# Row maxima of q transposed by TensorE instead of a DMA, and the first gating product read from SBUF, in a new order of the whole program

## The chip, the cores and the metric

The kernel runs on one core of a Trainium2 chip. The metric is the device time of one execution in microseconds (us), lower is better. Three executions of the kernel before took 317.10, 327.22 and 329.62 us (median 327.22). A profiled execution took 319.29 us, and its span, from the first to the last instruction, is 317.5 us. All durations below are from that profiled execution.

The engines are named as the profile names them: PE is TensorE (PEld its weight load), DVE is VectorE, ACT is ScalarE, POOL is GpSimd, SP is the engine that here only issues DMAs. Each engine executes its own instructions in the order in which they were written and waits, by semaphores, for what the others have to give it first.

## The reference

Two stages: a linear attention with exponential features, and a gated long convolution. Shapes: 8 batches, 8 heads, 576 rows, head width 64; the second stage has 576 rows by 512 channels.

```python
def phi(x):                       # q and k, w_phi is 64 x 128
    proj = x @ w_phi
    proj = proj - max(abs(proj), axis=-1)
    return concat([exp(proj), exp(-proj)])
kv  = phi(k).T @ v;   z = sum(phi(k))
x   = (phi(q) @ kv) / (phi(q) @ z + 1e-6)      # heads side by side: 576 x 512

x1, x2, x3 = split(x @ w_proj)                 # 512 -> 3 x 512
X2  = rfft(x2);  H = rfft(filter)
y   = x1 * irfft(X2 * H) * x3
out = y @ w_out
```

The first step of this change is in `phi(q)`: the maximum of each row has to be subtracted, and on the path of the transposed projection this is done by a matmul whose moving operand holds the maxima transposed. The second is in `X2 * H`, a complex product, of which the real and the imaginary part are each a sum of two products.

## The kernel before, in words

The program is one long list of words, `PLAN` (line 24), run through by `run` (line 967). A word such as `Pq,2,1@4` calls the method `Pq` with batch 2 and index 1 and gives it PSUM bank 4. The list was made by a planner and is the order of the work: each engine gets its instructions in the order of the words, so one word that waits holds everything that stands behind it on its engine. Loads from memory are issued by POOL (`load`, `loadh`, `w_load`), transposes by DMA and stores by SP, so these two queues follow the list as well. DMAs that are in flight at the same time share the 16 DMA engines.

For each of 8 batches the words are, in order of dependence:

- `load` brings q, k and v as bf16; `trh` (line 547) transposes a half of q or k by a DMA of SP. Batch 0 is transposed by PE (`T`, line 562, and `Te`).
- `Pk`, `Qn` and the short `Pkt`, `Qnt` project k and q by rows into PSUM; `maxk`, `maxq`, `maxkt`, `maxqt` reduce them to maxima of absolute values on DVE (line 654). `ex,k` are the exponentials of k on ACT, `em` the exponentials of the maxima of k, which `vs` on POOL multiplies into v; `KV` sums the products with v over the rows.
- The maxima of q take another way. `mhi` (line 674) rounds them to bf16 on ACT, `mlo` (line 677) makes the rest that bf16 lost, on POOL or DVE, both into the tile `mh`; `trm` (line 682) transposes `mh` to `mT` by a DMA of SP. `Pq` and `Pqt` (lines 609 and 624) project q with the features on the partitions and add, by matmuls with the constant `sel`, the negative maxima from `mT` to the same PSUM sums. `ex,q` and `exqt` are the exponentials of that.
- `NE`, `NEt` form numerator and denominator, `rc`, `xn`, `rct`, `xnt` divide on DVE, `trx` and `trxt` transpose the result by DMAs of SP.
- `fold` and `foldt` form even and odd parts for the transform; `X1`, `X2`, `X3` (with `X1t`, `X3t`) are the three projections, `X1e`, `X2e`, `X1te` copy them out of PSUM on ACT or DVE, and `tm`, `tmt` multiply x3 into x1.
- `F` (line 817) is the forward transform of x2, into two banks for index 0 and 1 and one bank for index 4. Two readers take the two banks: `Fe` (line 820) copies them as bf16 to the tile `C`, on ACT or DVE, and `m1` (line 823), always on DVE, multiplies them by the filter's `A` into `Y`. `m2` multiplies the other part of `C` by `B`, `m3` adds or subtracts the two; both are on POOL or DVE.
- `I` is the inverse transform; `Ie`, `Ip`, `Im` combine its halves, `ym` multiplies by x1 and x3, `O` (with `Oa`, `Ob`) is the last projection, `Oe` copies it out and `st` stores it, by two DMAs of SP.

The words of several batches are interleaved. Ahead of the first batch's second stage stand also the filter's transform (`filt_load`, `filt_fold`, `H`, `H_ev`) and the tables of sines (`gen_...`). The helper `port` (line 271) makes a POOL instruction wait for the last DVE instruction ahead of it that was handed to the helper; these are DVE instructions that work from SBUF to SBUF:

```python
        if eng == "DVE":
            self.hold = last or first
        elif eng == "POOL" and self.hold is not None:
            self.tc.add_manual_dep(
```

The functions that the change touches, and their caller:

Of the kernel before, what the change touches and what calls it, by code (L numbers as in the profile page):

```python
# [8 lines left out]
FP32 = mybir.dt.float32  # L9
# [3 lines left out]
ALU = mybir.AluOpType  # L13
# [23 lines left out]
Pq,0,0@0 ex,q,m,0,0@0 Qn,1,1@6 ex,q,p,0,0@0 Pq,0,1@2 ex,q,p,0,1@2 ex,q,m,0,1@2 gen_fwd trh,k,1,1
Pq,0,3@0 gen_fwd5 load,k,2 trh,k,2,1 trh,k,2,0 maxq,1,1@6 NE,0,0@4 ex,q,p,0,3@0 rc,0,0@4 xn,0,0@4
Pkt,1@6 maxkt,1@6 trx,0,0 load,v,1 ex,q,m,0,3@0 NE,0,1@2 rc,0,1@2 xn,0,1@2 trx,0,1 vs,POOL,p,0,1
vs,POOL,m,0,1 KV,0,1@4 KVe,DVE,0,1@4 exkt,m,1@6 exkt,p,1@6 em,m,1,0 Qn,1,0@0 maxq,1,0@0 Pq,0,2@2  # L40
ex,q,m,0,2@2 NE,0,3@4 ex,q,p,0,2@2 rc,0,3@4 xn,0,3@4 Pk,1,2@6 Qnt,1@0 em,p,1,0 w_load,proj,0
maxqt,1@0 mhi,1 filt_fold,POOL,0 Pqt,0@4 exqt,p,0@4 maxk,1,2@6 Pk,1,3@2 trx,0,3 filt_fold,POOL,2
load,q,2 NE,0,2@0 rc,0,2@0 xn,0,2@0 exqt,m,0@4 NEt,0@4 filt_fold,POOL,1 maxk,1,3@2 vs,POOL,m,1,0
H,1@0 ex,k,m,1,2@6 ex,k,p,1,2@6 mlo,POOL,1 trm,1 rct,0@4 xnt,0,0@4 em,m,1,1 xnt,0,1@4 H_ev,DVE,3@0
vs,POOL,p,1,0 gen_inv ex,k,m,1,3@2 H,0@6 H_ev,ACT,1@0 H_ev,DVE,0@6 ex,k,p,1,3@2 KV,1,0@4
KVe,DVE,1,0@4 trx,0,2 fold,POOL,0,1 H_fix H_ev,DVE,2@6 trxt,0 load,q,3 trh,q,2,0 Pq,1,0@0
ex,q,p,1,0@0 ex,q,m,1,0@0 Pq,1,1@2 ex,q,m,1,1@2 ex,q,p,1,1@2 w_load,proj,2 Pk,2,0@4 maxk,2,0@4
foldt,DVE,0,0 H,4@0 H_ev,DVE,4@0 ex,k,m,2,0@4 NE,1,0@6 rc,1,0@6 xn,1,0@6 X1,0,1@1 X1e,DVE,0,1@1
em,p,1,1 X1,0,0@2 X2,0,3@3 ex,k,p,2,0@4 Pk,2,1@6 ex,k,p,2,1@6 Qn,2,1@0 ex,k,m,2,1@6 foldt,POOL,0,1
late X2e,DVE,0,3@3 maxq,2,1@0 X2,0,4@4 X2e,DVE,0,4@4 X2,0,2@3 X2e,ACT,0,2@3 maxk,2,1@6 fold,POOL,0,0  # L50
X2,0,0@5 X2e,ACT,0,5@4 vs,POOL,p,1,1 X2,0,1@0 X1e,ACT,0,0@2 X2e,ACT,0,1@0 X2e,DVE,0,0@5 Qn,2,0@6
maxq,2,0@6 Pqt,1@2 exqt,p,1@2 exqt,m,1@2 trh,q,2,1 Qnt,2@4 maxqt,2@4 F,0,0@0 trh,q,3,0 Fe,ACT,0,0@0
load,k,3 Pkt,2@6 maxkt,2@6 F,0,1@2 X1,0,2@4 exkt,m,2@6 X1e,ACT,0,2@4 exkt,p,2@6 m1,0,0@0 Pq,1,3@0
ex,q,m,1,3@0 NE,1,1@4 Fe,DVE,0,1@2 ex,q,p,1,3@0 vs,POOL,m,1,1 KV,1,1@6 KVe,ACT,1,1@6 m1,0,1@2
em,p,2,0 Qn,2,2@2 rc,1,1@4 xn,1,1@4 maxq,2,2@2 trx,1,0 Pk,2,2@0 ex,k,p,2,2@0 Pq,1,2@4 trh,q,3,1
load,v,2 Qn,2,3@6 maxq,2,3@6 ex,q,m,1,2@4 mhi,2 m2,POOL,0,1 m2,POOL,0,0 X3,0,0@2 tm,0,0@2 X1t,0@3
X1te,ACT,0@3 maxk,2,2@0 F,0,4@6 m1,0,4@6 Pk,2,3@2 maxk,2,3@2 m3,POOL,0,0 ex,q,p,1,2@4 ex,k,m,2,2@0
X1,0,3@7 X1e,ACT,0,3@7 mlo,POOL,2 X3t,0@4 tmt,0@4 X3,0,3@6 tm,0,3@6 NE,1,2@0 rc,1,2@0 m3,POOL,0,1
I,0,0,0@7 vs,POOL,p,2,0 em,m,2,0 vs,POOL,m,2,0 em,p,2,1 vs,POOL,p,2,1 trm,2 ex,k,p,2,3@2 xn,1,2@0
trx,1,1 ex,k,m,2,3@2 NE,1,3@4 rc,1,3@4 trh,k,3,0 xn,1,3@4 X3,0,2@6 Qn,3,3@0 maxq,3,3@0 Ie,0,0@7  # L60
Pq,2,1@2 ex,q,m,2,1@2 ex,q,p,2,1@2 Qnt,3@4 maxqt,3@4 X3,0,1@7 em,m,2,1 Qn,3,0@0 maxq,3,0@0 Pq,2,0@4
ex,q,m,2,0@4 ex,q,p,2,0@4 NEt,1@2 trx,1,2 KV,2,0@0 KVe,ACT,2,0@0 rct,1@2 xnt,1,0@2 xnt,1,1@2 trx,1,3
tm,0,1@7 I,0,0,1@2 Ip,0,0@2 Im,0,0@2 I,0,1,0@3 Ie,0,1@3 tm,0,2@6 Pq,2,2@4 ex,q,p,2,2@4 NE,2,0@0
rc,2,0@0 ex,q,m,2,2@4 xn,2,0@0 vs,POOL,m,2,1 KV,2,1@2 KVe,ACT,2,1@2 trh,k,3,1 fold,DVE,1,1 Pq,2,3@6
ex,q,p,2,3@6 Qn,3,2@0 maxq,3,2@0 trxt,1 ex,q,m,2,3@6 trx,2,0 load,q,4 NE,2,1@4 rc,2,1@4 xn,2,1@4
trx,2,1 X2,1,2@2 X2e,ACT,1,2@2 w_load,out load,k,4 X2,1,3@3 X2e,DVE,1,3@3 I,0,2,0@0 Ie,0,2@0
fold,POOL,1,0 Qn,3,1@6 ym,POOL,0,0 maxq,3,1@6 Pk,3,0@4 ex,k,m,3,0@4 I,0,1,1@1 Ip,0,1@1 Im,0,1@1
X2,1,1@3 X2e,ACT,1,1@3 I,0,3,0@0 I,0,2,1@2 Im,0,2@2 NE,2,3@6 ex,k,p,3,0@4 Ie,0,3@0 X2,1,0@3
X2e,ACT,1,0@3 rc,2,3@6 foldt,POOL,1,0 xn,2,3@6 foldt,POOL,1,1 X2,1,4@1 X2e,ACT,1,4@1 X2e,ACT,1,5@1
Ip,0,2@2 mhi,3 Pqt,2@6 exqt,p,2@6 maxk,3,0@4 I,0,3,1@0 exqt,m,2@6 load,v,3 NE,2,2@2 X1,1,1@1  # L70
ym,POOL,0,1 Ip,0,3@0 Im,0,3@0 ym,POOL,0,2 mlo,DVE,3 F,1,0@4 rc,2,2@2 xn,2,2@2 F,1,4@0 m1,1,4@0
X1e,ACT,1,1@1 Fe,ACT,1,0@4 Pk,3,1@2 ex,k,p,3,1@2 ex,k,m,3,1@2 m1,1,0@4 load,k,5 F,1,1@6 m1,1,1@6
# [111 lines left out]
class Kernel:  # L184
# [824 lines left out]
```

## Time and profile before

| what | before |
|---|---|
| median of three executions | 327.22 us |
| profiled execution, its span | 319.29 us, 317.5 us |
| mean granted clock of PE | 0.946 of full speed |
| busy PE, DVE, ACT, POOL | 278.7, 250.6, 230.3, 220.3 us |
| DMA, mean over the span | 131 GB/s |
| SP's queue: transposes of x, k, q, maxima, rest of x | 32, 14, 14, 8, 8 |
| first matmul of `X2` (line 801) | 62.35 us after the span's start |
| last store issued | 313.27 us |

How to read it. A matmul's end is modelled, and matmuls overlap, so a busy PE can still have small gaps: what a row of matmuls costs is read from the starts. A group's line gives, after the bar, the busy us, the mean ns of one instruction, the idle time of the engine just before them and what ended it. The waits of an engine do no harm where that engine is not what the others wait for.

### The profile page before, as it was taken

To read this page: it belongs to the slowest core of one execution; us is meant where nothing else is said; L and a number is where in the kernel's file an instruction comes from. 1 tells how busy PE (TensorE), PEld (TensorE's weight loads), DVE (VectorE), ACT (ScalarE), POOL (GpSimd) and SP (SyncE) were. 2 spreads that over 40 slices of the span, in tenths; PEclk is the share of its full clock that TensorE was granted. 3 is DMA by queue.
4 is the path that set the end of the run, shared out by engine and by line. 5 is a ranking of instruction groups with operands and counts; after the bars stand their busy time and mean duration, and the time that the engine had idled before them with its cause. 6 is when DMAs were issued, how large, how long until landed. Compare 5 with 4: busy or idle time off the path is not lost.

```text
span 317.5 us, 9411 instructions
## 1 busy us (share of the span) xinstructions
PE 278.7 (88%) x3901; PEld 161.0 (51%) x3901; DVE 250.6 (79%) x415; ACT 230.3 (73%) x363; POOL 220.3 (69%) x171
## 2 busy tenths in 40 slices
PE   0553478899999999999799999999999999999991
PEld 0433365546675546466365555664565554654440
DVE  6994559999987988888679898987898866786750
ACT  5794378989888888885778957798768877635542
POOL 8697914799987786698589868956788566813230
PEclk9955559999999999999999999999999999999997
DMA  6999994899699996999969949565339310360346
GB/s 122 243 214 184 225 216 77 125 163 162 123 150 183 177 141 105 195 76 139 212 134 152 167 67 204 102 115 136 82 46 133 82 35 24 69 119 2 77 95 159
DMA packets 78666, 41.50 MB, mean 131 GB/s; under 512 B 58976, under 2 KB 73440, under 8 KB 78624
## 3 DMA queue, kind: packets, MB, share of 16 engines
q1 hardware_dynamic: 63808, 24.66, 45.3%
q0 software_dynamic: 14816, 16.25, 34.0%
q8 instruction: 30, 0.49, 0.7%
q14 instruction: 12, 0.10, 0.1%
HBM read 33.75 MB, written 9.44 MB: 136 GB/s over the span
## 4 chain that ended last, share of the span: by engine, by line
PE 64%; DMA 12%; DVE 11%; POOL 3%; SPq 3%; issue 3%; ACT 2%; POOLq 0%; DVEq 0%; ACTq 0%
PE ps L844 15%; DMA kT<-kn 9%; PE ps L895 8%; PE ps L801 7%; PE ps L936 7%; PE ps L458 5%; PE ps L709 4%; PE ps L730 4%; DVE mq L654 3%; DMA mT<-mh 2%; PE ps L851 2%; PE ps L587 2%; PE ps L621 2%; PE ps L442 1%; PE ps L615 1%
## 5 line engine op out<-in xcount | busy, mean ns | idle before, releaser
L844 PE MATMUL ps<-xT,wproj 128*128 128x512 bf16 x256 | 64.1, 379 | 0.2 <-DVE mq L654 0.2
L913 POOL TENSOR_TENSOR yT<-cv,x1s 128x576 bf16<-128x576 f32 x27 | 34.3, 1277 | 31.5 <-DVE cv L903 14.5
L654 DVE TENSOR_REDUCE mq<-ps 128x8 f32<-128x1024 f32 (+1 forms) x40 | 43.8, 1110 | 7.8 <-PE ps L594 6.8
L654 DVE TENSOR_REDUCE mk<-ps 128x8 f32<-128x1024 f32 (+1 forms) x40 | 44.2, 1112 | 3.7 <-PE ps L587 1.4
L694 POOL TENSOR_TENSOR vp<-vn,vp 128x1152 bf16<-128x1152 bf16 x16 | 34.4, 2150 | 9.2 <-ACT vp L688 7.1
L638 ACT ACTIVATE Ekm<-ps 128x1024 bf16<-128x1024 f32 x32 | 32.6, 1027 | 9.5 <-PE ps L587 5.8
L694 POOL TENSOR_TENSOR vm<-vn,vm 128x1152 bf16<-128x1152 bf16 x16 | 34.4, 2148 | 7.2 <-ACT vm L688 7.2
L638 ACT ACTIVATE Eqm<-ps 128x1024 bf16<-128x1024 f32 x32 | 32.7, 1025 | 5.1 <-PE ps L621 3.1
L936 PE MATMUL ps<-wout,yT 128*128 128x512 bf16 x144 | 36.2, 379 | 0.1
L832 POOL TENSOR_TENSOR t<-C,B 128x1024 bf16<-128x1024 bf16 x13 | 27.5, 2118 | 12.5 <-ACT C L714 9.5
L895 PE MATMUL ps<-inv,Y 128*128 128x288 bf16 (+1 forms) x192 | 36.0, 289 | 0.0
L638 ACT ACTIVATE Ekp<-ps 128x1024 bf16<-128x1024 f32 x32 | 32.9, 1028 | 3.7 <-DVE mk L654 2.2
L638 ACT ACTIVATE Eqp<-ps 128x1024 bf16<-128x1024 f32 x32 | 32.7, 1025 | 3.6 <-PE ps L621 2.9
L844 PEld LDWEIGHTS <-wproj 128*128 128x128 bf16 x256 | 23.1, 97 | 23.1 <-issue 0.2
L801 PE MATMUL ps<-wproj,eo 128*128 128x512 bf16 x128 | 31.1, 379 | 1.2 <-DVE KVs L716 1.2
L903 DVE TENSOR_TENSOR cv<-es,ps 128x288 f32<-128x288 f32 x64 | 26.5, 448 | 6.5 <-PE ps L895 5.2
L837 POOL TENSOR_TENSOR Y<-Y,t 128x1024 bf16<-128x1024 bf16 x14 | 29.6, 2124 | 2.3 <-DVE Y L827 1.1
L827 DVE TENSOR_TENSOR Y<-ps,A 128x1024 bf16<-128x1024 f32 (+1 forms) x24 | 24.7, 1041 | 4.6 <-PE ps L458 2.1
L881 DVE TENSOR_TENSOR x1s<-ps,x1s 128x512 bf16<-128x512 f32 x32 | 21.7, 686 | 5.1 <-PE ps L844 4.7
L714 ACT COPY o<-ps 128x512 f32<-128x512 f32 x29 | 17.0, 590 | 12.0 <-PE ps L936 7.7
L714 ACT CAST x1s<-ps 128x512 bf16<-128x512 f32 (+1 forms) x30 | 16.6, 552 | 10.3 <-PE ps L844 8.5
L895 PEld LDWEIGHTS <-Y 128*128 128x128 bf16 (+1 forms) x192 | 14.4, 96 | 18.3 <-issue 9.6
(153 smaller groups left out, 634.6 us busy)
## 6 DMA issues: line engine op xcount, KB each, us to landing
out_dram<-o SPq DMA_DIRECT2D x72, 128.0 KB, 2.4
vn<-in_v_dram POOLq DMA_DIRECT2D x8, 576.0 KB, 9.6
kn<-in_k_dram POOLq DMA_DIRECT2D x7, 576.0 KB, 8.6
qn<-in_q_dram POOLq DMA_DIRECT2D x7, 576.0 KB, 8.6
wproj<-in_moe_w_proj_dram POOLq DMA_DIRECT2D x3, 512.0 KB, 8.9
fl<-in_moe_filter_fft_dram SPq DMA_DIRECT2D x18, 64.0 KB, 5.1
kn<-in_k_dram POOLq DMA_DIRECT2D x2, 288.0 KB, 5.8
qn<-in_q_dram POOLq DMA_DIRECT2D x2, 288.0 KB, 7.9
```

The costliest lines, as they stand in the source:

```text
L638: self.nc.scalar.activation(e, self.db(), AF.Exp, bias=0.0, scale=1.0 if g == "p" else -1.0)
L654: self.nc.vector.tensor_reduce(out=out, in_=src, axis=AX.X, op=ALU.max, apply_absolute_value=True)
L694: self.port(eng, self.elem(eng).tensor_tensor(out=t[:, :, :, 0:64], in0=self.at("vn", b)[:, 2 * X:2 * X + 2], in1=t[:, :, :, 64:65].to_bro ...
L714: self.nc.scalar.copy(dst, src)
L801: self.mm(self.pb(0), eo[:, kt, 128 * c:128 * c + 128], w[:, kt, 512:1024], start=(kt == 0), stop=(kt == 3))
L832: self.port(eng, self.elem(eng).tensor_tensor(out=self.at("t2", b)[:, t, :], in0=self.at("C", b)[:, o, :], in1=self.at("B"), op=ALU.mult))
L837: self.port(eng, self.elem(eng).tensor_tensor(out=Y, in0=Y, in1=self.at("t2", b)[:, i:i + 3:2, :], op=ALU.add if i else ALU.subtract))
L844: self.mm(self.pb(0), w[:, kt, f0 + 128 * m:f0 + 128 * m + 128], x[:, kt, :], start=(kt == 0), stop=(kt == 3))
L895: self.mm(self.pb(0, 0, 288), y, t, start=(k == 0), stop=(k == 2))
L903: self.nc.vector.tensor_tensor(out=self.at("cv", 4 * b + m)[:, :, odd, :], in0=e, in1=o, op=ALU.subtract if odd else ALU.add)
L913: self.port(eng, self.elem(eng).tensor_tensor(out=self.at("yT", b)[:, m, 0:SEQ], in0=self.at("cv", 4 * b + m).rearrange("p j h t -> p (j h ...
L936: self.mm(self.pb(0), y[:, kt, 128 * j:128 * j + 128], w[:, kt, :], start=first and kt == ks[0], stop=last and kt == ks[-1])
```

## The change

Three things change at once.

`trm` is replaced by two words. `Tm` is a transpose by PE: a matmul against the identity, out of `mh` into a PSUM bank, like the words `T` that batch 0 uses for q and k. `Tme` copies the result to `mT`, on DVE for batches 0, 1, 2, 4 and 5 and on ACT for 3, 6 and 7.

`m1` of index 0 and 1 reads the copy in `C` instead of the PSUM banks, so it follows `Fe`, and the banks are free after `Fe`; as it has no operand in PSUM any more it may also be on POOL. Of the 16, ten are on DVE and six on POOL. `m1` of index 4 is as before.

The list of words is a new one throughout: 1,451 words instead of 1,443. The engines of many words are others. `Fe` is on ACT 10 times (13 before), `X1e` 19 (25), `X2e` of whole tiles 25 (18); `m2` is on POOL 8 times (13), `m3` 11 (14), `ym` 22 (27), `fold` 10 (8), `mlo` 7 (6). The rings of buffers are as before. Only the start of both lists is shown, up to the first words of batch 0's second stage; the tile of PSUM is called `banks` instead of `ps`.

```diff
 PLAN = """
-w_load,phi zeros w_phi,ACT loadh,k,0,1 gen_rows gen_cols,0 gen_turns,ACT,0 loadh,k,0,0 gen_cols,1
-gen_turns,DVE,1 gen_angles,1 gen_sin,1 gen_angles,0 gen_ident T,k,0,0,0@0 Te,ACT,k,0,0,0@0
...
-filt_load,SP,1 Pk,0,1@6 maxk,0,1@6 Qn,0,1@4 maxq,0,1@4 load,k,1 T,q,0,1,0@0 Te,DVE,q,0,1,0@0
-exkt,m,0@2 Qn,0,0@4 maxq,0,0@4 em,p,0,0 gen_sel T,q,0,1,1@1 Pk,0,3@2 maxk,0,3@2 load,q,1
...
-vs,POOL,m,0,0 KV,0,0@4 gen_five mhi,0 mlo,DVE,0 trm,0 Qn,1,3@0 KVe,DVE,0,0@4 ex,k,m,1,0@6
-ex,k,p,1,0@6 Pk,1,1@2 ex,k,m,1,1@2 ex,k,p,1,1@2 maxq,1,3@0 maxk,1,0@6 maxk,1,1@2 Qn,1,2@4 maxq,1,2@4
-Pq,0,0@0 ex,q,m,0,0@0 Qn,1,1@6 ex,q,p,0,0@0 Pq,0,1@2 ex,q,p,0,1@2 ex,q,m,0,1@2 gen_fwd trh,k,1,1
...
+w_load,phi w_phi,ACT zeros loadh,k,0,0 gen_rows gen_cols,1 gen_turns,DVE,1 gen_angles,1 gen_sin,1
+gen_cols,0 loadh,q,0,0 loadh,q,0,1 loadh,k,0,1 load,v,0 gen_ident T,k,0,0,1@0 filt_load,SP,0
...
+ex,k,p,0,1@0 load,q,1 T,q,0,1,0@6 Te,ACT,q,0,1,0@6 gen_turns,POOL,0 gen_angles,0 Te,DVE,k,0,1,1@5
+maxk,0,0@2 filt_load,SP,1 Pkt,0@4 maxkt,0@4 em,m,0,0 T,q,0,1,1@7 T,q,0,0,1@0 Te,DVE,q,0,0,1@0
+Te,DVE,q,0,1,1@7 Qnt,0@6 em,p,0,0 exkt,p,0@4 trh,q,1,0 exkt,m,0@4 trh,q,1,1 load,k,1 maxqt,0@6
+Qn,0,1@0 maxq,0,1@0 trh,k,1,0 Pk,0,3@2 Pk,0,2@6 ex,k,m,0,2@6 Qn,0,2@4 maxq,0,2@4 ex,k,m,0,3@2
+ex,k,p,0,2@6 gen_pads gen_sin,0 gen_sel gen_selx Qn,0,0@0 maxq,0,0@0 Qn,0,3@4 maxq,0,3@4 mhi,0
+vs,POOL,p,0,0 vs,POOL,m,0,0 maxk,0,3@2 maxk,0,2@6 em,p,0,1 em,m,0,1 mlo,DVE,0 KV,0,0@0 KVe,DVE,0,0@0
+Tm,0@6 ex,k,p,0,3@2 Tme,DVE,0@6 Pq,0,0@6 ex,q,p,0,0@6 ex,q,m,0,0@6 gen_five gen_inv Qn,1,0@0
+maxq,1,0@0 Pq,0,1@4 ex,q,m,0,1@4 ex,q,p,0,1@4 Qn,1,1@2 maxq,1,1@2 Pq,0,2@6 Qnt,1@0 maxqt,1@0
+trh,k,1,1 Qn,1,2@2 maxq,1,2@2 Pqt,0@0 ex,q,p,0,2@6 NE,0,0@4 gen_fwd5 NE,0,1@2 load,q,2 trh,q,2,0
+ex,q,m,0,2@6 exqt,m,0@0 rc,0,0@4 xn,0,0@4 trx,0,0 Pq,0,3@6 trh,q,2,1 Qn,1,3@4 exqt,p,0@0 rc,0,1@2
...
-        self.ps = self.psp.tile([128, 8, 512], FP32, name="ps")
+        self.banks = self.psp.tile([128, 8, 512], FP32, name="banks")
...
-    def trm(self, b):
-        self.nc.sync.dma_start_transpose(
-            out=self.at("mT", b), in_=self.at("mh", b).rearrange("p g h x -> p (g h x)"))
+    def Tm(self, b):
+        self.nc.tensor.transpose(self.turned(1), self.at("mh", b).rearrange("p g h x -> p (g h x)"),
+                                 self.at("ident"))
+
+    def Tme(self, eng, b):
+        self.copy(eng, self.at("mT", b), self.turned(1))
...
-    def m1(self, b, i):
-        t = slice(4, 5) if i == 4 else slice(i, i + 3, 2)
-        p = self.ps[:, self.bank:self.bank + (1 if i == 4 else 2), :]
-        a = {0: slice(0, 2), 1: slice(2, 0, -1), 4: slice(3, 4)}[i]
-        self.nc.vector.tensor_tensor(out=self.at("Y", b)[:, t, :], in0=p, in1=self.at("A")[:, a, :],
-                                     op=ALU.mult)
+    def m1(self, eng, b, i):
+        Y, A = self.at("Y", b), self.at("A")
+        if i == 4:
+            self.nc.vector.tensor_tensor(out=Y[:, 4, :], in0=self.pb(0), in1=A[:, 3, :], op=ALU.mult)
+            return
+        t = slice(i, i + 3, 2)
+        self.port(eng, self.elem(eng).tensor_tensor(
+            out=Y[:, t, :], in0=self.at("C", b)[:, t, :],
+            in1=A[:, slice(2, 0, -1) if i else slice(0, 2), :], op=ALU.mult))
```

Of the rest of the new list, the places that matter below are these. In batches 0 to 2 `Tm` stands right behind `mlo` or one `KV` after it; in the later batches some words of PE lie between them. Behind `Tm` of batch 1 stand `Pk,1,2`, `Qn,2,1` and `H`, behind that of batch 2 `X3`, `X3t` and `Pq`. SP's transposes of q of batch 2 stand ahead of the first `trx` of batch 0. `w_load,proj,1`, the weights of `X2`, is issued behind the loads of q, k and v of batch 2.

## The prediction

> **What bounds the kernel now.** I read the page's busy shares and slices first, then the window table, the chain of waits, and the groups that the change touches.
>
> ```profile
> PE 278.7 (88%) x3901; PEld 161.0 (51%) x3901; DVE 250.6 (79%) x415; ACT 230.3 (73%) x363; POOL 220.3 (69%) x171
> PE   0553478899999999999799999999999999999991
> PEclk9955559999999999999999999999999999999997
> 20.00:50.00 30.00, 16.01 (x321) 12.62 (x320) 17.67 (x26) 17.29 (x23) 19.65 (x15) 0.54 1.22 198
> 60.00:130.00 70.00, 69.44 (x1036) 39.97 (x1037) 62.50 (x100) 60.34 (x96) 59.10 (x42) 1.00 0.98 156
> 150.00:160.00 10.00, 7.68 (x89) 3.78 (x81) 5.49 (x10) 6.69 (x14) 6.17 (x7) 1.00 1.16 218
> 160.00:300.00 140.00, 139.80 (x1866) 78.12 (x1866) 115.27 (x186) 101.00 (x161) 94.96 (x63) 1.00 0.55 96
> ```
>
> A window row gives busy us of TensorE, weight load, VectorE, ScalarE and GpSimd, then granted clock, share of the DMA engines, GB/s. Three stages show. Until about 60 us TensorE is half idle and, from 20 to 50, clocked at 0.54. From 60 to 305 it has no hole but one of 2.3 us at 150:160. The last 12 us are evacuation and stores. To check how full 60 to 305 is I priced TensorE's work from the chain of waits, where four 512-column matmuls in a row take 0.86 us, a KV group 1.16 (72 matmuls in 55.50 to 56.66), an NE group 0.53: about 264 us for the program, 21 of it ahead of the first X2 (62.35 us), 243 behind it. Those 243 took until 311, 249 us. So **only the opening (41 us lost), one hole and the tail can give time**; the middle can only lose.
>
> ```profile
> 31.55 1.19 SPq L683 DMA_TRANSPOSE mT<-mh  x1
> 37.85 0.61 PE L621 MATMUL ps<-mT,sel 64*128 64x128 bf16 x8 [0.46 <-DMA mT<-mh]
>   PE ps L621: 0.7, 2
> DMA to landing us min/median/max: 2.2/3.5/7.2
> L827 DVE TENSOR_TENSOR Y<-ps,A 128x1024 bf16<-128x1024 f32 x16 | 19.3, 1219 | 2.8 <-PE ps L458 2.1 <-ACT C L714 0.6
> L832 DVE TENSOR_TENSOR t<-C,B 128x1024 bf16<-128x1024 bf16 x3 | 2.1, 686 | 0.0
> L837 POOL TENSOR_TENSOR Y<-Y,t 128x1024 bf16<-128x1024 bf16 x14 | 29.6, 2124 | 2.3 <-DVE Y L827 1.1 <-DVE t L832 0.7
> ```
>
> The two timeline rows show batch 0's maxima: complete at 26.35, issued by SP at 31.55 behind two q transposes, first read at 37.85. The next two lines are the answer for tile mT: over the whole run TensorE waited 0.7 us for it, twice.
>
> **Maxima by TensorE.** Removed: 8 SP transposes (median issue 1.18 us, 9.5 us of a queue that is not the bound) and those 0.7 us. Added: 8 Tm of the form of L568 (276 to 313 ns each, eight back to back in 1.01 us, so 0.13 in the flow): 1.0 us of TensorE, all on the path, for its queue has no slack. Added 8 Tme: the 128x128 copies of qT took 214 ns on VectorE and 306 on ScalarE, so 5 x 0.21 + 3 x 0.31 = 2.0 us beside other work. New wait: TensorE, in order, waits at Tm for mlo (7 of 8 on GpSimd). The orders leave TensorE work of 1.2, 0, 0, 1.9, 3.8, 5.0, 4.1 and 4.9 us between the places of mlo and Tm for batches 0 to 7. Behind Tm of batches 1 and 2 stand a projection and H, or X1 and X3 work; if GpSimd is one vs (2.15 us) late there, 4.3 us are lost. In batch 1 and 2 GpSimd's queue comes to mlo before VectorE has done the work listed ahead of it, so I take 0, bounds 0 to 4.3.
>
> **First product from C.** Sixteen VectorE products out of PSUM at 1.219 us (19.5) become ten from SBUF and six on GpSimd. No row shows m1 from C; the nearest is m2, same shapes and types: 0.686 on VectorE, 2.118 on GpSimd. So VectorE pays 6.9, saves 12.6. Counting all words that changed engine, by their rows, VectorE gets back: Fe +3 x 1.22, X1e +6 x 0.69, X2e -7 x 0.69 and one half +0.42, Oe +0.69, m2 +5 and m3 +3 x 0.69, ym +5 x 0.81, fold -2 x 0.69, foldt +0.4, Tme +1.1, the rest -1.2: +12.6 in all. **VectorE's total stays.** GpSimd: m1 +12.7, m2 -10.6, m3 -6.4, ym -6.4, fold +4.3, foldt -0.9, mlo +0.25, four turns (no row; 0.55 to 1.26 each) +2.2 to +5.0: down 2 to 5. ScalarE: -3.1, -3.5, +4.1, -2.2 and small ones, and two more table loads of 1.283 because the second sine now stands between exponentials: down about 1. The m1 that ran beside Fe now follows it: Fe 1.02, m1, m2, m3 at 0.69 instead of 1.22, 0.69, 0.69: +0.5 a batch. Between F and I of the last batch TensorE has 6 us of X1, X3 and O, which cover it; without that cover it costs 0.5 once.
>
> **The new opening.** All q maxima of batch 0 now stand ahead of the batch 1 ones, q1 is loaded before k1, and nothing of SP lies between mlo and the first Pq. VectorE ahead of mlo,0 from 11.2 us (where its generation ends): copies 2.2, angles 2.1, eight reductions 9.7, two tails 1.4 = 26.6. ScalarE ahead of mhi,0 from 13.2: seven exponentials 7.2, two copies 2.0, em and exkt 1.8, sine and its table 2.8 = 27.0. With mhi, mlo, KV, Tm, Tme the first Pq is ready at about 29, not 37.85. But batch 1 work that stood before it now follows. To the first X2: VectorE has 23 us left (52 without idle; it idled 5.6 of the 24.5 us from 37.85 to 62.35, so 57.7). SP has 13 transposes, not 14; those 14 took 20.44 to 56.2, 2.55 each; from a q1 landing at 20.4, as k1 landed, 13 end at 53.6, plus 2.8 landing and a 0.69 fold, 57.1. I take 57.5, bounds 54.5 (no idle) and 62.4 (the loads of q2 and k2, which SP now waits for ahead of the first xn transposes, come no earlier). Gain 4.85; but 1.8 us of TensorE work that preceded the first X2 (21.3 against 19.5 by count) now follows: net 3.0.
>
> **Sum**, against the profiled execution (319.29, span 317.5, 1.8 around it): 319.3 - 4.85 + 1.8 + 1.0 - 0.7 = **316.5**. The tail has one store group fewer behind F of batch 7 (two issues, 1.2 us), bounds -1.2 to +1.2, taken as 0. That execution lies 2.4% under the median 327.22 and inside 317.10 to 329.62; about 2% is what a measurement of this kernel can tell from no change.
>
> **A rule against the change.** One VectorE product reads two SBUF tensors while GpSimd works:
>
> ```profile
> 289.18 1.27 POOL L913 TENSOR_TENSOR yT<-cv,x1s 128x576 bf16<-128x576 f32 x1 [3.20 <-DVE cv L903]
> 290.01 1.05 DVE L913 TENSOR_TENSOR yT<-cv,x1s 128x576 bf16<-128x576 f32 x1
> ```
>
> It took 1055 ns where the median of the five is 754: 0.30 more. The Trainium skill (SBUF — State Buffer, "SBUF: two separate sides") says that a VectorE instruction with two SBUF inputs and a GpSimd instruction take an exclusive lock, and that the loser "fully blocks". By that rule an added instruction can lose up to a whole GpSimd one, against 0.30 by the row; the range below stands on rows alone.
>
> **Rivals.**
> - *The pair is worth what the opening allows at best, and the hole goes too* (0.27). First X2 at 54.5, net 6.0, and the 2.3 us of 150:160, where SP's q and k transposes and four more DMAs queue around an mT: 319.3 - 8.3 = **311**. For: TensorE full right after. Against: in the hole VectorE waits 3.7 us for xT and ScalarE 2.2 for the output ring, neither touched directly.
> - *Nothing* (0.07): mT was hidden (0.7 us of waits), VectorE's total stays, the loads still set the opening: **319.5**.
> - *VectorE and GpSimd collide* (0.28, the slower side). VectorE's large instructions with two SBUF inputs (fold, m1, m2, m3, ym) go from 18 to 39. Each of the 21 more can wait 0 to 2.15 us (the longest GpSimd row). With GpSimd busy 176 of the 240 us from 60 to 300, and half of 2.12 left when it is, 0.78 each, 16.3; VectorE is idle 16% there, which hides that share: 13.7. 316.5 + 13.7 = **330**. For: 60 to 130, where VectorE is 89% busy and ten of the 39 fall (four of the 18 did). Against: the helper that makes GpSimd wait for such an instruction let only one of 18 overlap. It decides over the opening from 0.13 us each on (2.8 / 21), and is 2% slower from 0.44.
>
> **How the numbers follow.** Forecast 0.38, its own range 312 to 320, of which 0.07 lies more than 2% under 319.3 (below 312.9). Faster: 0.27 + 0.07 = 0.34. Same: 0.31 + 0.07 = 0.38. Slower: 0.28. The range takes in the best opening with the hole and the tail bound (311 - 1.2 and a little: 308), and the collision's 330 less its far end; the scatter of single runs, +3.2% over the profiled one, reaches 327 from 316.5. So 308 to 329.
>
> **What would show it.** No L683 on SP; Tm idle under 0.5 us in sum and the first L621 near 29 us; the first L801 at 54 to 58; DVE products of 0.69 from C; a window 60 to 300 still with TensorE above 99%. Wrong, if VectorE rows of fold, m1, m2, m3, ym have means well over 0.69 and 0.75 (collision), if TensorE has holes before Tm or in 60 to 130, or if the first L801 comes after 60 (loads of q2 and k2).

## The result, and the profile after

| | kernel before | changed kernel |
|---|---|---|
| median of all executions | 327.22 us (15: 317.10 to 332.95) | 328.24 us (12: 325.89 to 336.56) |
| ratio, 95% interval | | 1.032 [1.028, 1.036] |
| forecast, range | | 316.5 us, 308 to 329 |

The medians lie 1 us apart and the ratio is 3.2%, because the ratio leaves out executions more than 1.5% above a kernel's quickest, and with the kernel before those are the many above 322 us. By the ratio the change costs about 10 us, where I forecast 3 us less. Over all 92 executions, those beside the experiments below included, the kernel before has a median of 322.8 us (315.66 to 333.59); by that the change costs about 5 us. None of the changed kernel's executions is under 325.89. The first profiled execution, 336.56 us, lies above all the others of the changed kernel, so a second profile of it, 327.74 us (span 326.0), is read here.

The page's busy times, its slices of TensorE and of the granted clock, then rows of the window table, with the columns named in the prediction:

```profile
PE 280.2 (86%) x3909; PEld 160.0 (49%) x3909; DVE 248.3 (76%) x429; ACT 229.4 (70%) x361; POOL 217.0 (67%) x169
PE   0576622389999999999999999999999999999991
PEclk9999975589999999999999999999999999999998
...
20.00:50.00 30.00, 16.20 (x372) 12.51 (x366) 24.39 (x39) 25.79 (x37) 25.36 (x21) 0.90 1.20 184
60.00:130.00 70.00, 66.16 (x952) 37.13 (x953) 57.52 (x91) 53.03 (x83) 46.02 (x36) 0.94 0.87 135
150.00:160.00 10.00, 10.00 (x116) 5.51 (x115) 8.62 (x18) 8.73 (x17) 8.76 (x5) 1.00 0.75 120
160.00:300.00 140.00, 139.67 (x1912) 77.95 (x1911) 111.99 (x192) 102.18 (x168) 99.33 (x63) 1.00 0.53 100
```

The hole at 150:160 is gone and the middle is full again from 80 us on; the opening is worse. Split up by TensorE's busy time in the windows 0 to 80, 80 to 300 and the rest, the 8.5 us between the spans (326.0 and 317.5) are: idle in 0 to 80 us 38.0 instead of 29.4 (+8.5), idle in 80 to 300 us 0.6 instead of 2.7 (-2.0), idle in the tail 7.2 instead of 6.7 (+0.5), busy time 280.2 instead of 278.7 (+1.5).

Where in the opening? Timeline rows of the changed kernel (start, us, engine, line, operation; in brackets the idle time and its releaser), with lines of the chain of waits for the landing and the first X2 (L806); the last block is a row of the kernel before:

```profile
26.59 0.29 PE L685 MATMUL banks<-ident,mh 128*128 128x128 bf16 x1 [1.34 <-DVE mh L681]
27.05 0.21 DVE L721 COPY mT<-banks 128x128 bf16<-128x128 bf16 x1
27.70 0.65 PE L623 MATMUL banks<-mT,sel 64*128 64x128 bf16 x8
...
36.52 8.31 SPq L550 DMA_TRANSPOSE qT<-qn  x1
49.04 1.31 SPq L402 DMA_TRANSPOSE fwd<-G  x1
50.44 7.52 SPq L773 DMA_TRANSPOSE xT<-xn  x1
...
47.88 0.81 POOL L502 DMA_DIRECT2D wproj<-in_moe_w_proj_dram  x1
48.67 0.75 POOL L534 DMA_DIRECT2D kn<-in_k_dram  x1
49.41 0.76 POOL L502 DMA_DIRECT2D wproj<-in_moe_w_proj_dram  x1
...
49.04 13.24 DMA fwd<-G
62.33 4.67 PE L460 MATMUL banks<-fe,fwd 32*128 32x512 bf16 x12 [10.65 <-DMA fwd<-G]
69.98 0.98 PE banks L806 x4
```

```profile
32.83 2.36 SPq L400 DMA_TRANSPOSE fwd<-G  x1
```

The first three rows are the new maxima: Tm at 26.6, copied at 27.05, the first Pq's maxima at 27.7, where the kernel before had 37.85. Then the first transpose of q2 holds SP for 8.31 us. The load of q2 is not the reason: it was issued at 23.16 and there at 30.8 us (the 7.0 us that SP's table of waits gives to a load of q belong to q1, from 14.1 to 21.1 us). Two transposes issued earlier, k1's second half and `gen_fwd5`, were still in flight and landed at 39.2 and 48.6 us; the table puts 6.4 us to TensorE. Which of the two held SP, the trace does not settle. Behind it stand the first xT, q2's second half, and `gen_fwd`, the transpose of the matrix for the Fourier transform: issued at 49.04, where the kernel before issued it at 32.83. Around it three loads start, 1.6 MB. It lands 13.24 us later, and for the last 10.65 of them TensorE, in order, stands before `H`, the filter's transform (L460). The first X2 comes at 70.0 instead of 62.35. In the execution of 336.56 us other tiles did it (kT 14.0 us, the folded xT 6.5) and X2 came at 75.9.

### The profile page after: what moved, and what is told of

Read it like the earlier page. It is cut to its first block, busy times and chain, and to the rows that moved or that the text cites. A ratio compares the mean times of both kernels' runs of the same rounds, so it can differ in the third digit from the quotient of the medians.

```text
span 334.8 us, 9424 instructions
## 1 busy us (share of the span) xinstructions
PE 285.8 (85%) x3909; PEld 163.2 (49%) x3909; DVE 248.5 (74%) x429; ACT 229.8 (69%) x361; POOL 217.1 (65%) x169
## 4 chain that ended last, share of the span: by engine, by line
PE 73%; DMA 15%; DVE 4%; SPq 2%; POOL 2%; issue 2%; ACT 0%; POOLq 0%; ACTq 0%; DVEq 0%
PE banks L852 17%; PE banks L806 9%; PE banks L944 9%; PE banks L903 8%; PE banks L460 7%; DMA kT<-kn 7%; PE banks L735 4%; PE banks L714 4%; DMA qn<-in_q_dram 4%; PE banks L859 2%; DMA xT<-xn 2%; SPq L550 2%; PE banks L617 2%; PE banks L589 2%; PE banks L623 2%; PE banks L596 2%
## 5 line engine op out<-in xcount | busy, mean ns | idle before, releaser
L852 PE MATMUL banks<-xT,wproj 128*128 128x512 bf16 x256 | 63.1, 379 | 0.0
L656 DVE TENSOR_REDUCE mk<-banks 128x8 f32<-128x1024 f32 (+1 forms) x40 | 44.0, 1111 | 16.2 <-PE banks L589 8.4
L656 DVE TENSOR_REDUCE mq<-banks 128x8 f32<-128x1024 f32 (+1 forms) x40 | 43.9, 1113 | 9.7 <-PE banks L596 4.6
L699 POOL TENSOR_TENSOR vp<-vn,vp 128x1152 bf16<-128x1152 bf16 x16 | 34.4, 2148 | 20.4 <-ACT vp L693 19.5
L640 ACT ACTIVATE Ekm<-banks 128x1024 bf16<-128x1024 f32 x32 | 32.7, 1028 | 9.9 <-DVE mk L656 7.7
L806 PE MATMUL banks<-wproj,eo 128*128 128x512 bf16 x128 | 33.6, 402 | 6.8 <-DVE eo L790 6.5
L944 PE MATMUL banks<-wout,yT 128*128 128x512 bf16 x144 | 35.9, 380 | 0.0
L903 PE MATMUL banks<-inv,Y 128*128 128x288 bf16 (+1 forms) x192 | 34.5, 289 | 0.3 <-DVE KVs L721 0.3
L640 ACT ACTIVATE Ekp<-banks 128x1024 bf16<-128x1024 f32 x32 | 32.6, 1026 | 2.7 <-PE banks L589 2.3
L640 ACT ACTIVATE Eqp<-banks 128x1024 bf16<-128x1024 f32 x32 | 32.8, 1028 | 2.4 <-PE banks L623 1.4
L640 ACT ACTIVATE Eqm<-banks 128x1024 bf16<-128x1024 f32 x32 | 32.7, 1028 | 0.8 <-PE banks L623 0.7
L911 DVE TENSOR_TENSOR cv<-es,banks 128x288 f32<-128x288 f32 x64 | 26.4, 450 | 7.8 <-ACT es L906 3.9
L790 POOL TENSOR_TENSOR eo<-xT 128x1024 bf16<-128x1024 bf16 x10 | 21.2, 2129 | 11.9 <-DVE eo L790 10.9
L845 POOL TENSOR_TENSOR Y<-Y,t 128x1024 bf16<-128x1024 bf16 x11 | 23.2, 2122 | 3.8 <-DVE t L840 3.2
L719 ACT COPY o<-banks 128x512 f32<-128x512 f32 x28 | 16.3, 590 | 10.4 <-PE banks L944 6.3
L903 PEld LDWEIGHTS <-Y 128*128 128x128 bf16 (+1 forms) x192 | 14.0, 96 | 17.6 <-issue 9.2
```

Of the source, the lines that this page charges most:

```text
L640: self.nc.scalar.activation(e, self.db(), AF.Exp, bias=0.0, scale=1.0 if g == "p" else -1.0)
L656: self.nc.vector.tensor_reduce(out=out, in_=src, axis=AX.X, op=ALU.max, apply_absolute_value=True)
L699: self.port(eng, self.elem(eng).tensor_tensor(out=t[:, :, :, 0:64], in0=self.at("vn", b)[:, 2 * X:2 * X + 2], in1=t[:, :, :, 64:65].to_bro ...
L719: self.nc.scalar.copy(dst, src)
L806: self.mm(self.pb(0), eo[:, kt, 128 * c:128 * c + 128], w[:, kt, 512:1024], start=(kt == 0), stop=(kt == 3))
L845: self.port(eng, self.elem(eng).tensor_tensor(out=Y, in0=Y, in1=self.at("t2", b)[:, i:i + 3:2, :], op=ALU.add if i else ALU.subtract))
```

## The experiments

**The opening: which transpose, and why it is late.** First `after_again`, the profile just read.

> The changed kernel once more, for a second profile: the first one, 336.56 us, lies 8 us above the median of its runs. If the late transposes of k1 in the opening (k1's second half 23.66 us from issue to landing, first X2 at 75.9 us) are what the change costs in every execution, this profile shows them too: a landing of 15 us or more, the first X2 after 65 us, and the rest of the program still about 250 us behind it. If they belong to that one execution only, the landing is under 9 us, the first X2 stands before 62 us, and the difference from the kernel before has to be looked for behind it.

Measured: 327.74 us, X2 at 70.0, k1's second half 12.0 us to landing (between the two expectations, 15 or more and under 9), 256 us behind X2. So both profiles of this kernel have the late opening, but the tile that is waited for changes. The next two move words alone.

```diff
 gen_five gen_inv
+gen_fwd                        (new_fwd, new_lean)
...
-gen_fwd ex,q,m,0,3@6 load,k,2
+ex,q,m,0,3@6 load,k,2
...
-w_load,proj,0 em,m,1,1 ... load,k,3 w_load,proj,2
+w_load,proj,0 load,v,2 em,m,1,1 ...                (new_lean: v2 later; k3, proj,2 behind X2,0,4)
```

> The changed kernel with one word moved: gen_fwd, the DMA transpose of the transform's matrix, stands behind gen_inv, ahead of k1's second half on SP, as in the kernel before, instead of behind the transposes of q2 and the first xT. In the second profile of the changed kernel it is issued at 49.0 us and lands at 62, and TensorE waits 10.6 us for it ahead of H. Theory (the late transform matrix is what the new opening costs): the wait of H for fwd goes, the first X2 comes before 64 instead of at 69.9 us, and the time falls by 4 to 9 us, to 319 to 324. Rival (the opening is bound by all the bytes that the DMA engines have to move; TensorE then waits for the next transposed tile, kT of batch 2 or xT): within 3 us of the changed kernel.

> As the one with gen_fwd early, and fewer bytes ahead of the first X2: the loads of v2 (behind the weights proj,0) and of k3 and the weights proj,2 (both behind the last X2 of batch 0) are later, 1.66 MB that the kernel before, too, loads only after its first X2 is near. Theory of the bytes: the first X2 at 56 to 61 us and 6 us or more faster than with gen_fwd early alone, 313 to 319. Rival (only the order on SP decides): the same as with gen_fwd early alone, within 2 us.

`new_fwd`: median 320.84 (318.68 to 327.71), ratio 1.010 [0.999, 1.022]. `new_lean`: 323.49 (320.02 to 329.36), 1.011 [0.999, 1.024]. So one word of 1,451, back in its old place, returns some 7 of the 10 us (by medians and by ratios of two sets of executions). That the bytes bound the opening is not borne out: 1.1 MB less ahead of X2 and a load of 0.6 MB later brought nothing more. Both profiles are of the longest execution of their kernel; that of `new_fwd` (325.9 us span) shows what comes next. TensorE's waits from 36 to 80 us (us, times, longest), and the chain:

```profile
PE banks L603 <- DMA kT<-kn: 6.0, 2, 3.1
PE banks L806 <- DVE eo L790: 4.0, 1, 4.0
PE banks L603 <- DMA qT<-qn: 3.4, 1, 3.4
...
55.92 14.38 DMA kT<-kn
70.35 0.40 PE banks L603 x4
```

A transpose of k2, issued right behind three loads (53.97 to 55.51 us), needs 14.38 us, and k2's projection stands between the first X2 and the second. Three kernels go on from there: `new_k2late`, made first, has the changed list with later loads; the other two have gen_fwd early too.

```diff
+w_load,proj,1 load,k,2 trh,k,2,1 trh,k,2,0 ... w_load,proj,0 load,v,2     (new_k2late, new_fwd_late)
+X2e,DVE,0,4@3 Pkt,2@6 maxkt,2@6 Pk,2,1@4 ... Pk,2,0@0 ...                (new_fwd_pk, new_fwd_late)
+X2,0,4@3 w_load,proj,2 load,k,3                                          (new_fwd_late)
```

> The changed kernel with two loads later in GpSimd's queue: k2 behind the weights proj,1 and v2 behind proj,0, with both transposes of k2 behind that load. Theory (the loads of batch 2 in flight with the transposes of k1 stretch those): k1's second half lands within 12 us, the first X2 comes 5 to 12 us earlier than in the changed kernel's own profile, and the time falls by 5 us or more, to 317 to 323. Rival (SP's order, q2's transposes ahead of the first xT ones, or the parts themselves): the first X2 stays within 3 us and so does the time.

> The changed kernel with gen_fwd early, as in new_fwd, and one more move: the projections of k of batch 2 (Pkt, Pk 1 and 0, with their maxima and exponentials) stand behind the last X2 of batch 0, not between the first and the second. In the profile of new_fwd TensorE waits for kT of batch 2 there, 3.1 us before the second X2, behind a transpose that landed 14.4 us after its issue. Theory (what is left of the loss is TensorE standing in order before a late transposed tile, though it has other work): 2 to 4 us faster than new_fwd, 315 to 318. Rival (the waits only move: xT of batch 0 and the product behind it are next): within 1.5 us of new_fwd, 319 to 321.

> As new_fwd_pk, with the loads later as well: k2 (and its transposes) behind the weights proj,1, v2 behind proj,0, k3 and proj,2 behind the last X2 of batch 0. Theory (order of waiting decides, and with the waits out of the way fewer bytes ahead of xT help): 1 to 3 us faster than new_fwd_pk, 313 to 317. Rival (the bytes only come later and kT of batch 2 is then waited for behind the X2): 2 us or more slower than new_fwd_pk.

`new_k2late`: 326.97 (326.47 to 330.86), ratio 1.033 [1.023, 1.043], with X2 at 59.6 us, ten earlier, and no gain: TensorE then waits 8.6 us for kT of batch 2, and 4.8 for fwd before. `new_fwd_pk`: 328.65 (323.48 to 338.04), 1.017 [1.008, 1.027]. `new_fwd_late`: 326.14 (324.11 to 326.37), 1.020 [1.015, 1.025]. The theories fell: each wait taken away came back at another tile (k1's second half, 10.8 us, in `new_fwd_pk`; eo 3.6 and qT 3.3 in `new_fwd_late`). `new_fwd_pk`, meant to better `new_fwd`, has a median 8 us above it (the ratios, 1.017 and 1.010, lie closer), which neither its theory nor its rival had; of `new_k2late`'s theory the earlier X2 came and the gain did not. The place of the first X2 alone says little. TensorE's idle time up to 80 us tells more (38.0 us in the changed kernel; 34.7, 33.9 and 33.0 in these three), but not all: `new_fwd`'s profile has 31.5 and the changed kernel's span, with TensorE busy for 286.5 us instead of 280.2.

Two more do the same in the old order:

```diff
-gen_fwd trh,k,1,1 Pq,0,3@0 ... trx,0,1 vs,POOL,p,0,1
+trh,k,1,1 Pq,0,3@0 ... trx,0,1 gen_fwd vs,POOL,p,0,1         (old_fwd_late)
...
-load,k,2 trh,k,2,1 trh,k,2,0 ... load,v,1 ... w_load,proj,0
+vs,POOL,m,0,1 load,v,1 ... load,q,2 load,k,2 trh,k,2,1 trh,k,2,0 w_load,proj,0     (old_quiet)
```

> The mirror image: the kernel before with gen_fwd later, behind the second trx of batch 0 (issued at about 50 instead of 32.8 us), nothing else. Theory (the place of this one transpose on SP is what the changed kernel loses most by): it lands at 57 to 63, H waits for it, the first X2 moves from 62.4 to 65 to 70 us, and the kernel is 3 to 8 us slower, its fastest executions at 320 to 325. Rival (fwd is only one of several equal waits): its fastest executions within 2 us of the kernel before.

> The kernel before with three loads later: v1 behind the second vs pair (30.6 instead of 23.6 us), k2 and the weights proj,0 behind q2 (36 us or later instead of 22.8 and 30.6), k2's transposes with k2. So between 24 and 30 us no load starts while SP's transposes of q1, k1 and the transform's matrix run. Theory (loads in flight with DMA transposes are what stretches these, from 8.9 us for k1's second half in the kernel before to 12 to 24 in other executions): that half lands within 7 us of its issue, the times of single executions lie within 2% of each other, and the fastest are not slower than those of the kernel before. Rival (the stretch comes without the loads, or moves behind them): landings of 9 us and more, the same spread of the single times, or a new wait for kT of batch 2.

`old_fwd_late`: 323.27 (319.53 to 326.51), ratio 1.008 [0.999, 1.018]; the first X2 at 61.25. The mirror image did not come, and it shows why. SP's row and TensorE's:

```profile
48.45 1.47 SPq L400 DMA_TRANSPOSE fwd<-G  x1
51.91 0.39 PE L458 MATMUL ps<-fe,fwd 32*128 32x512 bf16 x2 [0.88 <-DMA fwd<-G]
```

Issued at 48.45, as late as in the changed kernel, the same transpose is there after 3.4 us: no load had started since q2's at 36.49. In the changed kernel's first profile it was issued at 58.39 us, ahead of the next loads, and took 3.63. In both profiles of the changed kernel three transposes were in flight ahead of it; behind the last of them it needed 1.6 us more in the first and 9.9 in the second. And in `new_m1ps` below, which keeps the changed kernel's opening, it is issued at 48.97 among three loads (48.21, 49.01, 49.74) and lands after 14.07. So by these profiles the lateness has two parts: the place on SP, and **the loads that GpSimd starts just ahead of it** (13.24 us behind two loads and with a third). `old_quiet`: 324.98 (324.31 to 325.56), 1.018 [1.013, 1.022]. Fwd, issued at 30.0 with no load just started, lands after 5.7 us (7.2 in the kernel before); k1's second half, issued at 31.34 behind v1 (30.62) and with three more loads started from 36.4 on, needs 11.4 us, and TensorE waits 4.7 us for it and 4.7 for batch 1's mT. The theory held in the spread of the times and fell in the landing and in the time: the loads had only moved onto another transpose.

**The two parts, each alone.** In the old order:

```diff
-trm,0 ... (eight)                                        (old_tm)
+Tm,0@5 Tme,DVE,0@5 ... (between trm's place and the first Pq of the batch)
...
-m1,0,0@0 ...                                             (old_c: all sixteen behind their Fe)
+m1,DVE,0,0
...
-        self.port(eng, self.elem(eng).tensor_tensor(     (old_c_noport: m1 only)
+        self.elem(eng).tensor_tensor(
```

> The kernel before with the transposed maxima from TensorE, nothing else: each trm of the old list goes, Tm and Tme stand between its place and the first Pq of the batch. Theory (the new order's opening is what costs, not the parts): within 2 us of the kernel before, since 0.7 us of waits for mT go, 1.0 us of TensorE comes, and nothing else moves; Tm idle under 1 us in sum. Rival (the transposed maxima cost by a new wait of TensorE for mlo): 3 to 10 us slower, and the rows of Tm show the idle time.

> The kernel before with the first product read from C, all sixteen on VectorE, each behind its Fe; order and engines otherwise as before. Theory (opening): VectorE saves 16 x 0.53 = 8.5 us of busy time, but TensorE is full behind the first X2, so within 2 us of the kernel before, at best 3 faster. Rival (collision of VectorE and GpSimd over SBUF): fold, m1, m2, m3 and ym on VectorE come to means of 0.9 us and more, and the time is 5 us or more longer.

> The old order with all sixteen first products read from C on VectorE, as in old_c, which took 339 us; but these products are not handed to the helper that makes GpSimd wait for the last VectorE instruction handed to it. In old_c GpSimd waited 36 us for them. Theory (that wait is what the part costs in the old order): TensorE's holes behind 160 us go, 12 us or more of the 21 come back, 318 to 327, and VectorE's products are only a little slower than 0.745 us. Rival (the products are late whatever GpSimd waits for, since each now follows its Fe on ScalarE, or the two engines then collide over SBUF): still above 333, in the second case with means of 1 us and more for products, folds and ym on VectorE.

`old_tm`: 333.26 (323.89 to 334.62), no ratio; its fastest lies 2% above that of the kernel before in the same set, 316.95. Its profile (334.33) lost in the opening (TensorE busy 10.9 of 30 us in 20:50, before 16.0) and waits 1.3 us for one copy of mT by ScalarE; Tm itself waits 0.8 behind 80 us. Not settled more closely than "no gain". `old_c`: 339.25 (338.22 to 351.52), ratio 1.071 [1.060, 1.081]. GpSimd's waits from 80 us on, in old_c, and VectorE's group of the first product, in old_c and then in old_c_noport:

```profile
POOL yT L916 <- DVE Y L829: 20.1, 4, 7.9
POOL t L835 <- DVE Y L829: 8.2, 3, 4.0
POOL vp L694 <- DVE Y L829: 4.2, 1, 4.2
POOL vm L694 <- DVE Y L829: 3.9, 1, 3.9
```

```profile
L829 DVE TENSOR_TENSOR Y<-C,A 128x1024 bf16<-128x1024 bf16 x16 | 11.8, 745 | 10.6 <-ACT C L714 10.4
```

```profile
L829 DVE TENSOR_TENSOR Y<-C,A 128x1024 bf16<-128x1024 bf16 x16 | 19.2, 1206 | 8.1 <-ACT C L714 7.9
```

Here is the collision that I had as a rival, in its true form. A product from PSUM is not handed to `port`; one from SBUF is. So GpSimd's next instruction waits for a VectorE product that itself waits 10.4 us in sum for ScalarE's `Fe`: 36.4 us of new waits, and TensorE has 17.1 us of holes from 80 to 300 (before 2.7). This profile is of the longest execution, 351.52; TensorE also idles 40.2 us up to 80 us there, before 29.4, which fits its excess over the median. `old_c_noport` leaves that wait out: 331.49 (327.01 to 339.83), its fastest 3.4% above that of the kernel before (316.12). The holes shrink to 6.0 us, 11 of the 14.5 new ones come back; but now the products take 1206 ns instead of 745, 0.46 us more each. Both theories hold for a part. How they lose it shows instruction by instruction, here in one pair of rows (VectorE's product, GpSimd's m2):

```profile
203.52 2.62 DVE L829 TENSOR_TENSOR Y<-C,A 128x1024 bf16<-128x1024 bf16 x1
203.47 2.12 POOL L835 TENSOR_TENSOR t<-C,B 128x1024 bf16<-128x1024 bf16 x1
```

GpSimd's instruction starts first and ends at 205.59, the product at 206.14. Eight of the sixteen products start while a GpSimd instruction runs, and all eight end 0.54 to 0.55 us after that instruction's end; the others take 0.68 to 0.69 us. Where the product starts first, GpSimd's m2 takes up to 2.62 us instead of 2.12.

In the new order:

```diff
-Tm,0@6 ex,k,p,0,3@2 Tme,DVE,0@6                          (new_trm: all eight)
+trm,0 ex,k,p,0,3@2
...
-Fe,DVE,0,0@2 KVe,ACT,1,1@4 m1,DVE,0,0                    (new_m1ps: all sixteen, from PSUM)
+m1,0,0@2 Fe,DVE,0,0@2 KVe,ACT,1,1@4
```

> The changed kernel with the maxima transposed by SP's DMA again, each trm where Tm stands; the rest as in the changed kernel. Theory (transposing by TensorE saves the opening what SP's queue would take, and nothing later): the first Pq comes at 36 to 45 instead of 28 us, since its trm stands behind the transposes of q1 and k1, and the kernel is 3 to 10 us slower than the changed one. Rival (mT is hidden beside the other waits of the opening): within 2 us, since TensorE waits for fwd, kT and xT later in any case.

> The changed kernel with the first product read from PSUM on VectorE again, all sixteen, each ahead of its Fe; the rest as in the changed kernel. VectorE pays 16 x 1.22 = 19.5 us for 7.4, GpSimd is rid of 6 x 2.13. Theory (behind the opening TensorE is the bound and VectorE has room): 0 to 4 us slower than the changed kernel, 327 to 332. Rival (the part is what keeps VectorE from being the bound in this order): 6 us slower or more, with TensorE's holes in 80 to 300.

`new_trm`: 334.99 (333.94 to 336.83), ratio 1.058 [1.048, 1.068]: 7 us above the changed kernel. `new_m1ps`: 352.93 (349.34 to 357.08), 1.097 [1.089, 1.105]: 25 us above it. A wait of new_trm over the whole run, and three of new_m1ps from 80 to 340 us:

```profile
PE banks L622 <- DMA mT<-mh: 19.8, 4, 8.6
```

```profile
ACT C L718 <- DVE Y L831: 23.2, 10, 3.8
PE banks L616 <- ACT C L718: 3.5, 2, 2.7
PE banks L940 <- ACT C L718: 2.2, 1, 2.2
```

In this order neither part can be taken back alone. The theory of `new_trm` held, at its middle. Without Tm, TensorE waits 19.8 us for mT (0.7 in the kernel before, whose order had room for it). Without C, `Fe` comes behind a product of 1.22 us on VectorE (ScalarE waits 23.2 us for it in sum), the PSUM banks come free later, and TensorE waits for `C`: 14.8 us of holes from 80 to 300 instead of 0.6. VectorE has 12 us more of products to do there, so the 25 us are the price of both. That rival was right, my theory (0 to 4 us) wrong.

**The old opening with the new rest.** The first 207 words of the old list, then what is left in the new order.

```diff
 (old list up to) NE,1,0@6 rc,1,0@6 xn,1,0@6
-X1,0,1@1 ...
+trh,q,2,1 load,v,2 Qn,2,1@0 ... fold,DVE,0,0 ... late X2,0,0@6 ... (new list, without what is done)
```

> The first 207 words of the old order (up to the first X1, with the maxima of batches 0 and 1 still transposed by SP's DMA), then all that is left in the new order, with the maxima of batches 2 to 7 transposed by TensorE and the first product read from C; five PSUM banks are other ones. Theory (all that the change costs lies in the new order's opening; from the first X2 on the new order is 1 to 3 us better, without the hole at 150:160): the first X2 at 60 to 64 us, TensorE over 99% busy from 80 to 300, and 313 to 317, that is 0 to 1% faster than the kernel before. Rival (the new rest owes its fullness to work that its opening has already done): holes in 60 to 130 and 320 or more.

338.00 (328.70 to 342.27), no ratio; the fastest of the kernel before in this set 318.16. The theory fell. The profiled execution (338.45) lost much in the old opening itself (TensorE busy 10.5 of 30 us in 20:50; k1's second half 16.2 us to landing), and it has 3.5 us of holes in 80:130, where neither of the two kernels has 0.5; from 130 on it is as full as the changed kernel. I can't separate the two shares by this run.

**Towards a better kernel.** The maxima of batch 0 alone by TensorE, and the words behind them moved into the 5 us in which TensorE, VectorE and ScalarE of the kernel before idle for q1:

```diff
-mlo,DVE,0 trm,0 Qn,1,3@0 KVe,DVE,0,0@4 ex,k,m,1,0@6 ex,k,p,1,0@6 Pk,1,1@2 ...
+mlo,DVE,0 Tm,0@2 KVe,DVE,0,0@4 Tme,DVE,0@2 ex,k,m,1,0@6 ex,k,p,1,0@6 gen_fwd Pq,0,0@0 ...
...
-trh,k,2,1 trh,k,2,0 trx,0,0 trx,0,1                      (old_tm0_trx, old_tm01_trx)
+trx,0,0 trx,0,1 trh,k,2,1 trh,k,2,0
...
-trm,1 ... KV,1,0@4                                       (old_tm01_trx)
+Tm,1@3 KV,1,0@4 Tme,DVE,1@3
```

> The kernel before with the maxima of batch 0 alone transposed by TensorE, right behind KV, and the work that waits for them moved up: the first two Pq of batch 0 stand ahead of Qn,1,3, the third and the first two NE and xn among Qn,1,3, Pk,1,1 and Qn,1,2; SP's transposes of k2 still ahead of the first xT. Batches 1 to 7 as before. In the kernel before TensorE, VectorE and ScalarE idle 4.8 us (30 to 35 us) for q1 while the maxima are done at 26.4. Theory (part 1 is worth something where the opening waits, if the order follows and no DMA comes earlier): the first Pq at 31 to 32 instead of 37.9 us, and 1 to 4 us faster, its fastest executions at 313 to 316. Rival (the DMA engines set the opening's end whatever TensorE has done by then): its fastest executions within 1.5 us of the kernel before.

> As old_tm0, with SP's first two transposes of xT ahead of those of k2. Theory (SP's order decides when fold can start): the first X2 1 to 3 us earlier than in old_tm0 and the time 1 to 3 us shorter. Rival (the third and fourth xT, which follow the second half of Pq, end last): the same as old_tm0 within 1 us.

> As old_tm0_trx, with the maxima of batch 1 transposed by TensorE too, ahead of its first KV, so that SP has no mT between the third and the fourth xT of batch 0 (1.18 us of issue there in old_tm0_trx, 51.64 to 52.9). Theory (SP's order in the opening is worth what its issues take): the fourth xT is issued 1.2 us earlier, the first X2 comes up to 1.2 us earlier, and the fast executions lie at 314.5 to 317. Rival (the transposes' landing, not their issue, ends the opening; or Tm of batch 1 waits for a GpSimd that is late): the same as old_tm0_trx within 0.5 us, or slower.

> old_tm0_trx once more, against the kernel before. Theory (0.7% faster, by the 4 to 5 us in which the engines no longer idle for q1 and by the earlier xT): its fast executions at 314 to 318, a ratio between 0.986 and 1.000. Rival (the first measurement caught more of the quick openings than is the rule; the DMA engines' rate decides): a ratio of 1.00 to 1.01, with executions up to 335 as many as in the kernel before.

`old_tm0`: 323.99 (318.91 to 326.57), ratio 1.004 [0.995, 1.013]. `old_tm0_trx`: 316.69 (315.70 to 335.41), 0.993 [0.986, 1.001], and again as `old_tm0_trx_b`: 320.70 (316.79 to 331.66), 1.002 [0.997, 1.006]. `old_tm01_trx`: 327.46 (322.22 to 329.70), no ratio, its fastest 2% above that of the kernel before (315.66). In the profile of old_tm0_trx the first maxima are read at 31.08 instead of 37.85 us, TensorE is busy 17.6 of the 30 us instead of 16.0, and the first measurement looked like a gain; the second, larger one shows none. No version here is shown to beat the kernel before.

## Why the prediction was wrong, point by point

- **The new opening: this step failed.** I put the first X2 at 57.5 us, bounds 54.5 to 62.4; it came at 70.0. The step was "13 transposes, 2.55 each, from a q1 landing at 20.4". The count and the start were right (13 issues from 21.11 to the last xT), the spacing was not: they ended at 65.09 us, 3.4 us each, and that xT landed at 66.2 us where I had 56.4. Three issues have half of the time: k1's second half 6.42 us, q2's first half 8.31, the second xT 7.52, each with two transposes still in flight ahead of it. (My 2.55 was also miscounted: the 14 of the kernel before ended at 54.11, 2.40 each; 56.2 is the end of a fifteenth.) And I had not followed `gen_fwd` at all, though it is moved past q2's transposes and `H` stands ahead of the first X2: a term put at nothing, which was 10.65 us of TensorE. Moving it back returned some 7 us. The duration was wrong as well: behind loads just started a transpose lands in 13 to 14 us, not in the 2.8 I took.
- **The upper bound** stood on "the loads of q2 and k2", at the old place of X2. They were not it: q2 was there at 30.8 us and k2 at 35.8, before SP came to their transposes (36.52 and 58.06).
- **TensorE's work behind the first X2**, +1.8: not separable; the split above shows +1.5 us of busy time in all.
- **Eight Tm, 1.0 us on the path, and the waits of mT, -0.7**: Tm takes 219 ns (median), and TensorE waits 0.4 us for mT in the whole run. The first Pq came at 27.7, forecast 29. The wait at Tm, taken as 0 with bounds 0 to 4.3, was 2.7 us, both in the opening (1.3 for mlo of batch 0, 1.4 for the xn that frees the bank of batch 1's Tm).
- **The first product**: forecast 0.686 and 2.118, measured 0.744 (ten on VectorE) and 2.125 (six on GpSimd); m2, m3 and fold 0.686, 0.690, 0.685. VectorE's total stayed, as forecast: 248.3 us, before 250.6. What I missed is that, in an order made for it, C also frees the banks early; `new_m1ps`, which takes back that and VectorE's relief together, is 25 us slower.
- **The collision (rival, 330 us)**: the changed kernel's median is near that number, but not for that reason. Of the ten products one pays: 1.258 us, ending 0.54 after a GpSimd instruction that ran when it started; the others take 0.68 to 0.69. ym has a mean of 781 ns where the kernel before had 814. The mechanism is real, and its price was well bounded: with `port` left out the products take 0.46 us more. The rule I weighed against the row (the Trainium skill, SBUF — State Buffer, "SBUF: two separate sides") speaks of a full block, and the rows of `old_c_noport` agree with it: a product that starts second ends 0.54 to 0.55 us after the GpSimd instruction, 2.62 us in the longest case. The mean of 0.46 us is small because half of the products met no GpSimd instruction or came first; my row with 0.30 us fits as well: that product ends 0.61 us after GpSimd's instruction, which was mostly over when it started. With `port` the price is paid as waits of GpSimd instead, and the new order has places for them.
- **The hole at 150:160** goes, as in the rival of the full opening: -2.0 us in 80 to 300. **The tail**: +0.5, inside -1.2 to +1.2.
- **The sign I set for being wrong**, the first X2 after 60, is the one that came; the reason I gave for it, the loads of q2 and k2, is not.

## What to carry to other kernels

Where a list is reordered, follow every DMA by its place in its queue: what stands ahead of it now, what that waits for, and which instruction of an in-order engine stands before its landing. A count of issues times a mean duration hides a single transpose that is moved behind a wait, and a table of waits gives no times: look up when a wait was before it is made the cause. An edit that helps in one order can cost 20 us in another, so "the part" has no price without the order; and an operand that moves from PSUM to SBUF may bring a wait in a helper that only looks at SBUF instructions.

## What the runs showed of the hardware

Transposes of the same kinds move at very different rates. From the DMA tables: SP's queue in the kernel before, 36 to 50 us, and in the changed kernel's first profile, 35 to 45 us (packets, MB, share of 16 engines; q0 are GpSimd's loads):

```profile
q1 hardware_dynamic: 7140, 1.77, 77.3%
q0 software_dynamic: 886, 0.94, 39.8%
```

```profile
q1 hardware_dynamic: 1557, 0.39, 110.0%
q0 software_dynamic: 260, 0.29, 35.6%
```

Per us of the 16 engines that is 0.164 MB of transposes and 0.169 of loads (1.77 / (0.773 x 14), 0.94 / (0.398 x 14)) against 0.035 and 0.081. Other profiles of both orders have such stretches too (old_c 90 GB/s in 35 to 45 us), at about the same place and with transposes of fwd, k1 and q1 or q2 and loads in flight together. With the loads moved away (`old_quiet`) the executions lie within 0.4% of each other, which fits, but four of them don't settle it, and why such a mixture runs at 197 GB/s in one execution and at 68 in another stays open. It is not the program alone: `old_tm0_trx` was profiled twice, and the spans are 314.5 and 325.3 us, with TensorE idle for 26.4 and 35.4 us up to 80 us and the first X2 at 61.58 and 71.02. Whether the spread of the kernel before, 315.66 to 333.59, comes from its opening too is not shown: one execution of it was profiled. TensorE's granted clock, 0.54 in the kernel before's 20:50 and 0.90 in the changed kernel's, went the other way than the time.
